# Windowed attention and a squared-ReLU layer on one core: a clamp in the adding instruction, paired squares, V half copies by DMA, and tokens 1024 to 1535 by half-size products

## The chip, the cores and the metric

The kernel runs on one NeuronCore of a Trainium2 chip. The metric is the device time of one execution in microseconds. The engines are named as in the profile: PE is TensorE's matrix products and PEld its weight loads, DVE is VectorE, ACT is ScalarE, POOL is GpSimd, SP is SyncE, which here only issues transfers. Each engine works through its own queue in order, and a wait at the head of a queue holds everything behind it.

## What is computed

The reference, cut to what matters, has two stages. The first is attention in a window of 32 positions to each side, over 8 batches, 8 heads, 576 positions and 64 channels a head. The second is a two-layer network on the 4608 tokens that come out.

```
scores = scale * np.matmul(q, k.transpose(0, 1, 3, 2))
mask = np.abs(pos[:, None] - pos[None, :]) <= 32
attn = softmax of scores where mask
x = (attn @ v), as 4608 tokens x 512
h = x @ w_in                     # 512 -> 2048
r = np.maximum(h, 0.0)
out = ((r * r) @ w_out)          # 2048 -> 512
```

## The kernel before

Attention works through 24 groups of 192 tokens (three to a batch). POOL loads a group's K, Q and V and turns them to bf16 on the way (`load_qk`, L377; `load_v`, L415). The windows of two groups overlap: half of the first V tile of a group equals half of the second tile of the group before. For the 16 groups that are not the first of their batch, that half is copied inside the core, by VectorE (L410) or ScalarE (L412), instead of being loaded.

K and Q have to be turned so that channels lie along the partitions. For the first NTG = 9 groups TensorE does this with products against an identity (`turn_pe`, L463), and VectorE or ScalarE moves the result from PSUM (L476, L477). For the other groups a DMA does it, issued from SP (`turn_dma`, L491). Likewise the result of attention is turned by TensorE for the first NXT = 9 groups (L630, L636, moved by L644 or L646) and by SP's DMA for the others (`xturn`, L649, L652). Between these lie the scores (L531), the exponential by ScalarE (L554), the mask by VectorE (L562), the product with V (L590) and the division (L604, L608). For the first NSPLIT = 6 groups the two windows of a group are masked one by one, for the others together.

The first layer works on 512 tokens at a time, over 2048 columns. Two forms exist. The plain one (`mm1`, L690) does products of 128x192, 128x256 or 128x512 over four slices of the contraction; ScalarE takes max(h, 0) from PSUM to bf16 (L665, or VectorE at L664) and VectorE or ScalarE squares it (L660, L659). It is used for tokens 0 to 1535; tokens 1024 to 1535 come as products of 128x512, in pairs of two PSUM banks (`PAIR`). The other form (`mm1s`, L770) splits tokens, contraction and columns in halves and gets the eight half products from seven (Strassen's scheme in Winograd's form). It needs four differences of the inputs (L742) and of the weights (L730). It is used for the six stretches of 512 tokens from 1536 on, each in four blocks m of 256 + 256 columns. In a block, two banks X and Y take the seven products in the order 1, 2, 6, 5, 7, 3, 4, and the results are taken out in between:

- after product 1 the bank X is copied to Y (L809 or L810);
- after product 2, X holds the first result: `one` takes max(h, 0) (L665) and squares it, 512 wide;
- after products 6 and 5, Y and X are copied to SBUF in fp32 (L670);
- after products 7 and 3, `fused` adds the copy to Y and to X on VectorE and writes bf16 (L794); when both are there, one instruction of 1024 clamps them at zero (L800 on VectorE or L801 on ScalarE) and one squares them;
- after product 4, Y holds the last result: `one` again, 512 wide.

The second layer uses the same scheme of seven products (`strassen`, `product`, L917; its sums at L885, its additions at L949) for all but the first 512 tokens, which go through L835. Some of its blocks, and those of the first layer, begin with a product of zeros over the whole second bank (`wash`, L895), where a mark "w" in the order asks for it. Stores to DRAM go out through SP or ScalarE (L847, L848).

The order of everything is written out by hand in the string ORDER: for each recorded operation an engine letter (P, A, D, G, S) and a due time, and for each buffer a slot. The due times come from a plan and decide only the order in each engine's queue; on the chip every operation starts when its waits are over. While TensorE has nothing to do in the first microseconds it runs products of zeros (`fill`, L299).

Of the kernel before, what the change touches and what calls it, by code (L numbers as in the profile page):

```python
# [2 lines left out]

# [18 lines left out]
    MM1S=(1536, 2048, 2560, 3072, 3584, 4096),  # L22
# [8 lines left out]
    NTG=9,  # L31
# [3 lines left out]
    NXT=9,  # L35
    NSPLIT=6,
# [20 lines left out]
    ALTB=300,  # L57
)
# [170 lines left out]
def dve(n, fast=True):  # L229
    return 153 + (0.52 if fast else 1.04) * n  # L230


class Gen:
# [7 lines left out]
    def alloc(self):  # L241
# [31 lines left out]
        if cfg["MM1S"]:  # L273
            self.SW = [sb(f"sw{i}", [128, 2, 1024], BF16) for i in range(4)]
            self.XS = [sb(f"xs{i}", [128, 2, 256], BF16) for i in range(4)]
# [125 lines left out]
    def load_v(self, b, g, key, after=None):  # L401
        G, NV = 3 * b + g, self.cfg["NV"]
        vt = self.V[G % NV]
        for j in range(2):
            k0 = 192 * g - 32 + 128 * j
            lo, hi = max(k0, 0), min(k0 + 128, S_)
            if self.vcopy(G) and j == 0:
                lo += 64
                vs, vf = self.V[(G - 1) % NV][64:128, 1, :, 0:64], vt[0:64, 0, :, 0:64]
                self.p.rec("DVE", lambda e, vs=vs, vf=vf: e.tensor_copy(vf, vs), reads=[("v", (G - 1) % NV, 1)], writes=[("vc", G % NV)],  # L410
                           key=key + 2, dur=290, name=f"vc{b}{g}",
                           alt=("ACT", act(512), lambda e, vs=vs, vf=vf: e.activation(vf, vs, ACTF.Copy)) if self.cfg["ALT"] else None,  # L412
                           bias=self.cfg["ALTB"])
# [319 lines left out]
    def mm1s(self, t0, key):  # L733
# [5 lines left out]
        b11, b12, b21, b22 = xt[:, 0:2, r:r + 256], xt[:, 0:2, r + 256:r + 512], xt[:, 2:4, r:r + 256], xt[:, 2:4, r + 256:r + 512]  # L739
        for i, a, b, rd in ((0, b12, b11, st[0] + st[1]), (1, b22, xs[0][:], st[1] + [("xs", 0)]),  # L740
                            (2, b22, b12, st[1]), (3, b21, xs[1][:], st[0] + [("xs", 1)])):
            p.rec("DVE", lambda e, o=xs[i][:], a=a, b=b: e.tensor_tensor(o, a, b, ALU.subtract), reads=rd, writes=[("xs", i)],  # L742
                  key=key, dur=dve(512), name=f"xs{i}.{t0}")
        tag = lambda f, h: [("gt", (t0 // 64 + 4 * h + x) % (GRING // 64), d) for x in range(4) for d in f]
        for m in range(4):
# [46 lines left out]
            def fused(src, tg, u, y, kk, nm, hh=hh, add=add):  # L792
                hs = lambda y=y: self.rt(hh)[:, 512 * y:512 * y + 512]
                add.append(p.rec("DVE", lambda e: e.tensor_tensor(hs(), src(), self.oe(u), ALU.add), reads=[tg, u],  # L794
                                 writes=[(hh, y)], key=kk, dur=dve(512, False), name=nm, uses=[v, hh], after=add[0] if y else None))
                if y or not cfg["FP"]:
# [3 lines left out]
                    p.rec("DVE", lambda e: e.tensor_scalar(src2(), src2(), 0.0, None, ALU.max), reads=rd, writes=rd, key=kk, dur=153 + 0.26 * c,  # L800
# [6 lines left out]

            prod(1, ks[0])
# [3 lines left out]
            one(X, xtag, rt, lo, ks[1], f"{t0}.{m}")  # L812
# [80 lines left out]
    def wash(self, e, v):  # L893
        if v.wash:
            e.matmul(self.bank(v, 1), self.ZZ[:, 0:128], self.ZZ[:, 0:512], start=True, stop=True)  # L895
# [190 lines left out]
D900 G1350 A1170 D2200 D5546 D9773 D10213 D10698 D7178 D9553 D11762 D7058 D7598 D10413 D11962 D9453 D5746 D17653 D5256  # L1086
D4966 D1100 D1800 D9993 D10808 D2000 D7378 D9253 D18439 D38379 D42315 D48333 D30870 D48923 S1350 D6458 S900 D4366
G2488 G1700 G4852 G3276 G5640 G4064 G6428 G7956 A1600 A8036 A2050 A7416 G7168 G9388 A14797 G8696 G11052 G10272 G11936
G14196 G17484 G19880 G19100 A20153 G12716 G13408 G20660 G22228 P7128 D7733 P8149 D8701 P9323 A9958 D11076 P10902
A11926 D13121 P12451 D12921 D13806 D14562 P15127 D15742 D16012 P16197 P16768 A17208 P10560 A11112 P11327 D12062 P13044  # L1090
A13769 D15057 P13859 A16107 D17753 P15812 D16698 D16968 A18022 P18772 D19242 D19512 P19032 P20347 D20883 P14284 A15399
P8746 A12954 P16998 A18631 D20198 P19922 A20755 D21967 P21297 D21767 D22653 A23417 P24197 D24667 D24937 P24457 P27062
A27502 G15812 G14976 G18264 G16648 G21440 G29120 P26667 A28812 P31252 D31857 P32967 A33735 D34952 P18112 A19659 P34916
A35551 D37008 P19262 A22922 A24520 P42969 D43856 D44741 D46664 P47949 D48433 D49043 P48634 P50153 D50648 P20637 D23338
P22877 A28317 A31435 P24687 A25557 P27292 D28162 D30990 P31647 D39217 G25324 G26852 G23796 G23008 D48633 G33156 G33848
P45589 A46819 P43229 A43781 P36669 D39839 D41762 P48209 A48844 D49962 P23537 D28715 P50383 A51018 D53131 P27952 A29733
D30318 P51233 D51885 D52155 A53074 P54597 D55067 D55953 P54857 P57743 D58183 P21557 A22427 D33714 D41077 D42415 D43170
D44056 D45979 D55267 D65040 P22217 A24025 A26052 P25347 A26867 D25623 D37694 D26378 D27134 D32476 D36323 D35637 D40391
P26007 A32250 A37979 P32307 A33240 G26112 G24584 G28380 G27640 D52841 G30840 G44088 P45299 A46111 P46795 D47295 P33392
D34399 A36579 P48864 A49872 D51200 P28612 A30940 P50808 A52046 D54369 P30592 D33162 D38664 P53677 D56638 D56908 A57664  # L1100
P58633 D59354 D59624 P61205 P61435 D61875 P39921 A40791 P29932 A42101 D53816 P29272 A32745 P34052 P38193 P40581 P44435
A45509 A84798 P35341 A38794 A41286 P36001 A37484 G31532 G38378 G30004 G35520 G58298 G44876 P55087 A55768 P57348 D58736
P42309 D45426 D47781 P60555 A61415 A62533 D63822 P52153 A53682 P53937 A55274 D62428 P66663 D67167 D68590 A69481 P71217
D72383 D72653 P73101 P74641 D75081 P37329 P41445 P43571 P45931 A47634 A68310 P55482 A56690 P58893 A59763 D63270 P51493
A54177 P57973 A58843 D70796 P59895 D61152 G39214 G34732 G32368 G43300 D62980 G36356 G42416 P59553 D60600 P57006 D57594
P39057 P47085 P49289 P52813 A54672 A92023 P73331 A74201 D81590 P64276 A65136 A66254 D67372 P62529 A63613 P68670 D69275
D69545 D70301 P70957 D71427 D71697 P72641 P72871 D74509 P66923 A70089 A72187 P63403 D65726 P64926 D66481 A67282 P56142
P61665 P65799 P68930 A74695 S89327 P71477 A73215 G64554 G59826 G62094 G46452 D60310 G45760 G75739 P70667 A71479 P72351
D73338 P74871 D76318 D78751 G62834 G48131 G48967 G47295 G65294 G63670 P73991 A75297 A76415 D77533 S67856 S69146 P67797
A68880 P78984 D79454 D80339 D81095 P83561 D84578 D85464 P100060 P100290 D102613 P69794 A70877 D73824 P80107 P80971  # L1110
A82373 D87520 D79654 D86149 D75633 D84778 D82142 P83821 P84695 A85779 P88206 P89080 D96479 A91421 A114133 P89954
P93074 A94158 P94208 P95082 A101298 P100780 P101654 D103165 A111183 P102528 P104052 D106283 A112550 P104926 P105800
A106884 S107575 P75744 P76607 A77681 A95788 G56480 G55692 G66082 G61306 A87456 G75047 G81159 P77471 A78821 A81345
# [112 lines left out]
```

## Time and profile before

| what | value |
|---|---|
| runs of the kernel | 289.16, 287.22, 288.34 us; median 288.34 |
| profiled execution | span 287.0 us from the first to the last instruction; the page gives no other time of it |
| instructions | 7773 |
| granted TensorE clock, mean | 0.999 |
| first-layer seven-product blocks | 24, with 672 products of 128x256 (L770) |
| plain first-layer products | 256 of 128x192, 64 of 128x256, 59 records of 128x512 (L690) |

The profiled execution's span is 1.3 us under the median of the runs, which also count what lies around the span. A row of a group names line, engine, operation, the tiles written and read, their shapes and the count; then the busy time in us and the mean duration of one in ns; then how long the engine stood idle just before them and on what. A row of the stages gives, for each stretch of the span, the busy time and the instruction count of each engine, the granted clock of TensorE, the DMA share and the rate. Matrix products overlap, so their durations (some 273 ns for one of 128x256) are longer than the distance from one to the next.

### The profile page before, as it was taken

To read this page: it belongs to the slowest core of one execution; us is meant where nothing else is said; L and a number is where in the kernel's file an instruction comes from. 1 tells how busy PE (TensorE), PEld (TensorE's weight loads), DVE (VectorE), ACT (ScalarE), POOL (GpSimd) and SP (SyncE) were. 2 spreads that over 40 slices of the span, in tenths; PEclk is the share of its full clock that TensorE was granted. 3 is DMA by queue.
4 is the path that set the end of the run, shared out by engine and by line. 5 is a ranking of instruction groups with operands and counts; after the bars stand their busy time and mean duration, and the time that the engine had idled before them with its cause. 6 is when DMAs were issued, how large, how long until landed. Compare 5 with 4: busy or idle time off the path is not lost.

```text
span 287.0 us, 7773 instructions
## 1 busy us (share of the span) xinstructions
PE 279.1 (97%) x3137; PEld 234.6 (82%) x3151; DVE 238.0 (83%) x438; ACT 215.7 (75%) x328; POOL 115.0 (40%) x153
## 2 busy tenths in 40 slices
PE   8999999999999999998999999999999999999995
PEld 8879866787756688886898888888888888888884
DVE  4787797989887798996899989998989978898721
ACT  2787666857868787887887889988887688798620
POOL 8999867194498052076235912605000000000000
PEclk9999999999999999999999999999999999999999
DMA  9999999999999999999999996989941612200233
GB/s 143 165 193 185 204 173 156 156 113 152 119 158 175 190 112 147 190 115 163 163 154 134 151 166 144 132 180 118 145 98 46 130 34 61 75 0 2 73 112 110
DMA packets 162915, 37.57 MB, mean 131 GB/s; under 512 B 150080, under 2 KB 162368, under 8 KB 162880
## 3 DMA queue, kind: packets, MB, share of 16 engines
q0 software_dynamic: 113728, 17.93, 87.7%
q1 hardware_dynamic: 44432, 15.34, 29.8%
q10 hardware_dynamic: 4720, 3.80, 5.1%
q8 instruction: 25, 0.41, 0.6%
q14 instruction: 10, 0.08, 0.1%
HBM read 36.70 MB, written 9.44 MB: 161 GB/s over the span
## 4 chain that ended last, share of the span: by engine, by line
PE 78%; DMA 10%; POOL 6%; DVE 2%; issue 2%; ACT 1%; ACTq 0%; DVEq 0%; POOLq 0%
PE ps L917 31%; PE ps L770 24%; PE ps L690 9%; PE ps L835 4%; POOL raw L377 4%; PE ps L590 3%; DMA w<-in_moe_w_in_dram 3%; PE ps L531 3%; DMA kq<-raw 3%; DMA v<-in_v_dram 2%; POOL v L415 2%; DMA xt<-xa 2%; PE ps L463 1%; DVE rt L794 1%; PE ps L630 0%
## 5 line engine op out<-in xcount | busy, mean ns | idle before, releaser
L665 ACT ACTIVATE rt<-ps 128x512 bf16<-128x512 f32 (+2 forms) x81 | 48.4, 606 | 17.6 <-PE ps L690 7.3
L670 ACT ACTIVATE oe<-ps 128x512 f32<-128x512 f32 x72 | 42.0, 595 | 22.2 <-PE ps L917 15.1
L554 ACT ACTIVATE e<-ps 128x1024 bf16<-128x1024 f32 x48 | 48.8, 1022 | 6.8 <-PE ps L531 5.0
L377 POOL DMA_DIRECT2D raw<-in_q_dram x46 | 36.7, 809 | 42.3 <-DMA kq<-raw 39.0
L377 POOL DMA_DIRECT2D raw<-in_k_dram x46 | 36.8, 816 | 27.2 <-DMA kq<-raw 20.8
L917 PE MATMUL ps<-w,gt 128*128 128x256 bf16 x384 | 47.0, 273 | 0.0
L690 PE MATMUL ps<-xt,w 128*128 128x192 bf16 (+2 forms) x379 | 46.4, 271 | 0.6 <-DMA w<-in_moe_w_in_dram 0.2
L415 POOL DMA_DIRECT2D v<-in_v_dram x48 | 38.6, 814 | 12.4 <-ACT v L412 10.0
L917 PEld LDWEIGHTS ps<-w,gt 128*128 128x128 bf16 x384 | 36.6, 98 | 4.9 <-issue 0.2
L770 PE MATMUL ps<-xs,sw 128*128 128x256 bf16 x288 | 39.9, 272 | 0.0
L690 PEld LDWEIGHTS ps<-xt,w 128*128 128x128 bf16 x384 | 32.4, 98 | 8.8 <-ACT v L412 0.3
L659 ACT ACTIVATE gt<-rt 128x512 bf16<-128x512 bf16 (+2 forms) x51 | 38.7, 777 | 0.3
L794 DVE TENSOR_TENSOR rt<-ps,oe 128x512 bf16<-128x512 f32 x48 | 32.9, 688 | 5.1 <-PE ps L770 3.8
L917 PE MATMUL ps<-ts,gt 128*128 128x256 bf16 x256 | 31.9, 273 | 0.0
L562 DVE TENSOR_TENSOR pt<-e,mask 128x2048 bf16<-128x2048 bf16 (+1 forms) x30 | 30.2, 1007 | 1.9 <-ACT e L554 1.4
L917 PE MATMUL ps<-ts,ss 128*128 128x256 bf16 x256 | 31.7, 273 | 0.0
L770 PEld LDWEIGHTS ps<-xs,sw 128*128 128x128 bf16 x288 | 27.4, 98 | 3.3 <-ACT oe L670 0.2
L770 PE MATMUL ps<-xt,w 128*128 128x256 bf16 x192 | 27.2, 273 | 0.2
L917 PEld LDWEIGHTS ps<-ts,ss 128*128 128x128 bf16 x256 | 24.7, 98 | 3.2
L660 DVE TENSOR_TENSOR gt<-rt 128x1024 bf16<-128x1024 bf16 (+2 forms) x49 | 26.4, 557 | 0.8 <-ACT rt L665 0.7
L917 PEld LDWEIGHTS ps<-ts,gt 128*128 128x128 bf16 x256 | 24.5, 98 | 3.2 <-DVE oe L949 0.3
L770 PEld LDWEIGHTS ps<-xt,w 128*128 128x128 bf16 x192 | 18.1, 98 | 3.3 <-ACT ps L809 0.4
(70 smaller groups left out, 405.2 us busy)
## 6 DMA issues: line engine op xcount, KB each, us to landing
out_dram<-oe SPq DMA_DIRECT2D x23, 256.0 KB, 3.5
out_dram<-oe ACTq DMA_DIRECT2D x13, 256.0 KB, 4.4
v<-in_v_dram POOLq DMA_DIRECT2D x16, 128.0 KB, 5.5
w<-in_moe_w_in_dram POOLq DMA_DIRECT2D x4, 512.0 KB, 9.8
w<-in_moe_w_out_dram POOLq DMA_DIRECT2D x4, 512.0 KB, 16.4
raw<-in_q_dram POOLq DMA_DIRECT2D x18, 96.0 KB, 5.3
raw<-in_k_dram POOLq DMA_DIRECT2D x14, 112.0 KB, 5.3
raw<-in_q_dram POOLq DMA_DIRECT2D x14, 112.0 KB, 6.9
```

Source lines behind the costliest of these rows:

```text
L377: self.p.rec("POOL", lambda e, j=j, dst=dst: e.dma_start(dst, s[j]), writes=[self.rtag(t, b, g, j)], dma=(f"{t}{G % self.cfg['NRAW']}{j}", ...
L415: self.p.rec("POOL", lambda e, j=j, lo=lo, hi=hi, k0=k0: e.dma_start(vt[lo - k0:hi - k0, j, :, 0:64], self.v[b, :, lo:hi, :].rearrange("h ...
L554: last = self.p.rec("ACT", lambda e, ef=ef, v=v: e.activation(ef(), self.bank(v, 0, 2), ACTF.Exp, scale=0.125), reads=[v], writes=tags, ke ...
L562: self.p.rec("DVE", lambda e, pf=pf, ef=ef, mb=mb, n=n: e.tensor_tensor(pf(y=0, n=n), ef(y=0, n=n).rearrange("p (w h q) -> p w h q", w=n, ...
L659: alt = ("ACT", act(c), lambda e: e.activation(dst, src(), ACTF.Square)) if self.cfg["ALT"] else None
L660: self.p.rec("DVE", lambda e: e.tensor_tensor(dst, src(), src(), ALU.mult), reads=rd, writes=wr, key=key, dur=dve(c), name=name, alt=alt, ...
L665: return self.p.rec("ACT", lambda e: e.activation(dst(), src(), ACTF.Relu), reads=rd, writes=wr, key=key, dur=act(c), name=name, alt=alt, ...
L670: self.p.rec("ACT", lambda e: e.activation(dst(), src(), ACTF.Copy), reads=rd, writes=wr, key=key, dur=act(c), name=name, alt=alt, bias=se ...
L690: mm = e.matmul(ht[:, n * x:n * x + n], self.W1[:, ft, 128 * d:128 * d + 128], self.XT[:, ft, r:r + n], start=(ft == 0 and x == 0), stop=( ...
L770: mm = e.matmul(bk[:, 256 * x:256 * x + 256], lhs(k, 256 * m + 128 * x), rhs[:, k, :], start=start and x == 0 and k == 0, stop=(k == 1), s ...
L794: add.append(p.rec("DVE", lambda e: e.tensor_tensor(hs(), src(), self.oe(u), ALU.add), reads=[tg, u], writes=[(hh, y)], key=kk, dur=dve(51 ...
L917: mm = e.matmul(op[:, 256 * y:256 * y + 256], lhs[:, l0[0] + k, a:a + 128], rhs[:, r0 + k, c0:c0 + 256], start=start and y == 0 and k == 0 ...
```

## The change

It has seven parts, and a new ORDER over all of them, of which the diff shows the first line; the old one has two marks "w", the new one has one.

1. **Clamp inside the addition** (`AS`): the addition of `fused` becomes VectorE's TENSOR_ADD_SAT, which computes max(min(a + b, s0), s1) with s0 the largest fp32 number and s1 = 0. The clamping instruction goes.
2. **Squares in pairs** (`ZP`): a block's first result (`one`, after product 2) shares a buffer with the sum after product 7, and the sum after product 3 shares one with the last result (after product 4). Each pair is squared by one instruction of 1024. Before there were squares of 512, 1024 and 512.
3. **Merged differences** (`XM`): two of the four input differences become one instruction of 1024.
4. **V half copies by DMA** (`VD`): the 16 copies are transfers issued from SP, of 64 partitions with their padding columns, instead of copies by VectorE or ScalarE.
5. **Tokens 1024 to 1535** go from the plain form to the seven-product form.
6. **Group 8, the ninth,** has K, Q and its result turned by SP's DMA (NTG and NXT from 9 to 8).
7. **Groups 3 to 5** have both windows scored and masked together (NSPLIT from 6 to 3).

A wider block (`wide`) comes with the change but is not called (`WIDE=()`); it is left out here.

```diff
-    MM1S=(1536, 2048, 2560, 3072, 3584, 4096),
+    MM1S=(1024, 1536, 2048, 2560, 3072, 3584, 4096),
-    NTG=9,
+    NTG=8,
-    NXT=9,
-    NSPLIT=6,
+    NXT=8,
+    NSPLIT=3,
+    AS=1,
+    VD=1,
+    ZP=1,
+    XM=1,
+    WIDE=(),
...
+            self.XSA = sb("xs", [128, 4, 2, 256], BF16)
+            self.XS = [self.XSA[:, (0, 2, 1, 3)[i], :, :] for i in range(4)]
...
+                if self.cfg["VD"]:
+                    vs, vf = self.V[(G - 1) % NV][64:128, 1, :, :], vt[0:64, 0, :, :]
+                    self.p.rec("SP", lambda e, vs=vs, vf=vf: e.dma_start(vf, vs), reads=[("v", (G - 1) % NV, 1), ("vset", (G - 1) % NV), ("vset", G % NV)],
+                               writes=[("vc", G % NV)], dma=(f"vc{G % NV}", G), key=key + 2, dur=450, move=(4, 60), name=f"vc{b}{g}",
+                               slack=self.cfg["TSLACK"])
-                self.p.rec("DVE", lambda e, vs=vs, vf=vf: e.tensor_copy(vf, vs), reads=[("v", (G - 1) % NV, 1)], writes=[("vc", G % NV)],
...
+        if cfg["XM"]:
+            both = [bass.AP(xt, o, [[4 * RING, 128], [x, 2], [RING, 2], [1, 256]]) for o, x in ((r + 256, 2 * RING), (r, 256))]
+            p.rec("DVE", lambda e: e.tensor_tensor(self.XSA[:, 0:2, :, :], both[0], both[1], ALU.subtract), reads=st[0] + st[1],
+                  writes=[("xs", 0), ("xs", 2)], key=key, dur=dve(1024), name=f"xs0.{t0}")
...
+            def pair(z, y, src, tg, u, kk, nm, held, v=v, lo=lo, hi=hi):
+                zf = lambda: self.rt(z)[:, 512 * y:512 * y + 512]
+                if u is None:
+                    held.append(self.relu(zf, src, [tg], [(z, y)], kk, "r" + nm, 512, uses=[v, z], after=held[0] if y else None))
+                else:
+                    held.append(p.rec("DVE", lambda e: e._custom_dve(TENSOR_ADD_SAT, out=zf(), in0=src(), in1=self.oe(u), s0=3.4028234e38, s1=0.0),
+                                      reads=[tg, u], writes=[(z, y)], key=kk, dur=dve(512, False), name=nm, uses=[v, z], after=held[0] if y else None))
+                if y:
+                    o = 256 if u is None else 0
+                    dst = bass.AP(gt, lo[0] * GRING + rg + o, [[16 * GRING, 128], [(hi[0] - lo[0]) * GRING + 256 - 2 * o, 2], [GRING, 2], [1, 256]])
+                    self.square(lambda: self.rt(z).rearrange("p (y d t) -> p y d t", y=2, d=2), dst, [(z, 0), (z, 1)],
+                                tag(lo, int(o > 0)) + tag(hi, int(o == 0)), kk, "g" + nm, 1024, uses=[z])
...
             prod(2, ks[1])
-            one(X, xtag, rt, lo, ks[1], f"{t0}.{m}")
+                pair(za, 0, X, xtag, None, ks[1], f"{t0}.{m}", ha)
...
             prod(7, ks[4])
-            fused(Y, ytag, p5, 0, ks[4], f"c22.{t0}.{m}")
+                pair(za, 1, Y, ytag, p5, ks[4], f"c22.{t0}.{m}", ha)
             prod(3, ks[5])
-            fused(X, xtag, u2, 1, ks[5], f"c12.{t0}.{m}")
+                pair(zb, 0, X, xtag, u2, ks[5], f"c12.{t0}.{m}", hb)
             prod(4, ks[6])
-            one(Y, ytag, rt2, hi, ks[6], f"{t0}.{m}b")
+                pair(zb, 1, Y, ytag, None, ks[6], f"{t0}.{m}b", hb)
...
 ORDER = """
-D900 G1350 A1170 D2200 D5546 D9773 D10213 D10698 D7178 D9553 D11762 D7058 D7598 D10413 D11962 D9453 D5746 D17653 D5256
...
+D850 G850 A22521 D3755 D1300 D2605 D3555 D4665 D1500 D3115 D8849 D4775 D8729 D5880 D10316 D4895 D1900 D15584 D4375
...
```

More of the change, by code (lines that the diff above doesn't have):

```diff
@@ L2 @@
 from concourse import mybir
+from concourse.dve_ops import TENSOR_ADD_SAT
 ALU = mybir.AluOpType
@@ L744, in mm1s @@
         tag = lambda f, h: [("gt", (t0 // 64 + 4 * h + x) % (GRING // 64), d) for x in range(4) for d in f]
+        if t0 in cfg["WIDE"]:
+            for m in range(2):
+                self.wide(t0, key + 4 * m, m, (b11, b21, b22), st, tag)
+            return
         for m in range(4):
@@ L894, in wash @@
         if v.wash:
-            e.matmul(self.bank(v, 1), self.ZZ[:, 0:128], self.ZZ[:, 0:512], start=True, stop=True)
+            for i in range(v.n // 2, v.n):
+                e.matmul(self.bank(v, i), self.ZZ[:, 0:128], self.ZZ[:, 0:512], start=True, stop=True)
     def product(self, g, i, key, v):
@@ L1091 @@
[L1091 to L1110, printed above, removed]
```

272 lines of the change are left out of this document (188 added, 84 removed), and 11 rows, old and new, of the table ORDER.

## The prediction

> **What bounds the kernel now.** I read the page first (its busy times), then the busy time by stage, the waits of TensorE, the chain of waits, and last the groups of instructions with the shapes kept apart.
>
> ```profile
> span 287.0 us, 7773 instructions
> PE 279.1 (97%) x3137; PEld 234.6 (82%) x3151; DVE 238.0 (83%) x438; ACT 215.7 (75%) x328; POOL 115.0 (40%) x153
> ```
> ```profile
> core 0: us, PE busy (x) PEld busy (x) DVE busy (x) ACT busy (x) POOL busy (x), PEclk, DMA share, GB/s
> 20.00:80.00 60.00, 59.38 (x750) 46.89 (x756) 51.43 (x101) 44.02 (x67) 40.53 (x54) 1.00 1.81 158
> 80.00:110.00 30.00, 29.18 (x300) 20.75 (x302) 25.88 (x43) 23.53 (x29) 18.31 (x24) 1.00 1.82 157
> 110.00:140.00 30.00, 28.54 (x308) 24.47 (x306) 26.03 (x47) 24.09 (x38) 10.31 (x13) 1.00 1.56 151
> 140.00:283.00 143.00, 142.88 (x1489) 125.24 (x1490) 121.44 (x207) 111.61 (x180) 26.85 (x35) 1.00 0.77 105
> 180.00:190.00 10.00, 10.00 (x116) 8.70 (x114) 9.23 (x16) 9.40 (x16) 3.79 (x5) 1.00 1.79 134
> ```
> ```profile
> PE ps L770 <- DVE rt L794: 1.3, 1, 1.3
> ```
> ```profile
> 11.65 9.21 DMA w<-in_moe_w_in_dram
> 37.84 2.59 PE ps L835 x12
> 126.16 5.83 DMA xt<-xa
> 246.94 9.61 PE ps L770 x88
> 265.28 18.35 PE ps L917 x168
> ```
>
> TensorE is the bound. From 20 to 283 us it is idle 0.62 + 0.82 + 1.46 + 0.12 = 3.0 us, at full granted clock (1.00). Its one wait of weight, 1.3 us, lies where the chain passes through a transpose that landed late (126.16, 5.83 us): VectorE stood waiting for it with an addition behind. VectorE and ScalarE are both busy, but after 140 us they keep TensorE waiting for next to nothing. So an instruction taken from them there pays nothing by itself; a product taken from TensorE pays in full. A busy TensorE is not one at its peak, so I price products by their spacing in the chain: 128x512 products cost 2.59/12 = 215.8 ns, 128x256 products 9.61/88 = 18.35/168 = 109.2 ns.
>
> **The change part by part: TensorE.**
>
> ```profile
> L690 PE MATMUL ps<-xt,w 128*128 128x512 bf16 x59 | 14.2, 379 | 0.4 <-issue 0.2
> L895 PEld LDWEIGHTS ps<-zz 128*128 128x128 bf16 x2 | 0.2, 98 | 0.0
> ```
> ```profile
> 70.81 0.42 PEld L463 LDWEIGHTS ps<-ident,raw 80*128 80x128 bf16 x8
> 72.49 0.42 PEld L463 LDWEIGHTS ps<-ident,raw 80*128 80x128 bf16 x8
> 100.50 0.42 PEld L630 LDWEIGHTS ps<-ident,xa 128*128 128x128 bf16 x4
> 100.89 0.27 PEld L636 LDWEIGHTS ps<-ident,xb 128*128 128x128 bf16 x4
> ```
>
> - Tokens 1024 to 1535: 16 column tiles x 4 = 64 products of 128x512 go (the group shows 59, some records being missing), 64 x 215.8 ns = 13.81 us. In come 4 blocks x 7 products x 4 = 112 of 128x256, 112 x 109.2 ns = 12.23 us: **-1.58 us**.
> - Of the two washing products (L895, a 128x512 each) one mark "w" is left in the new order: **-0.2 us**.
> - The ninth group (number 8): 16 turns of K and Q go (70.81 and 72.49: 0.42 us of weight loads per eight, the last 98 ns of each overlapping what follows, so some 0.33 us; 0.65 together) and 8 turns of its result (from 100.50 to 100.89 + 0.27 less one load, some 0.5; gaps in it put the true price nearer 0.4): **-1.05 us**, with 0.8 and 1.2 as ends.
>
> TensorE sum: -2.83 us. The two scores of groups 3 to 5 in one piece leave the products as they are.
>
> **VectorE and ScalarE.**
>
> ```profile
> L801 ACT ACTIVATE rt<-rt 128x1024 bf16<-128x1024 bf16 x8 | 8.4, 1055 | 1.0 <-DVE rt L794 1.0
> L800 DVE TENSOR_SCALAR rt<-rt 128x1024 bf16<-128x1024 bf16 x16 | 6.9, 440 | 0.2
> L794 DVE TENSOR_TENSOR rt<-ps,oe 128x512 bf16<-128x512 f32 x48 | 32.9, 688 | 5.1 <-PE ps L770 3.8 <-ACT oe L670 0.4 <-ACT gt L659 0.2
> L660 DVE TENSOR_TENSOR gt<-rt 128x1024 bf16<-128x1024 bf16 x21 | 14.2, 683 | 0.0
> L660 DVE TENSOR_TENSOR gt<-rt 128x512 bf16<-128x512 bf16 x18 | 7.2, 417 | 0.0
> L412 ACT ACTIVATE v<-v 64x512 bf16<-64x512 bf16 x9 | 5.6, 622 | 1.0 <-DMA v<-in_v_dram 0.9
> L410 DVE COPY v<-v 64x512 bf16<-64x512 bf16 x7 | 2.0, 290 | 0.2
> L665 ACT ACTIVATE rt<-ps 128x1024 bf16<-128x1024 f32 x8 | 8.2, 1023 | 2.5 <-PE ps L690 2.4
> L670 ACT ACTIVATE oe<-ps 128x512 f32<-128x512 f32 x72 | 42.0, 595 | 22.2 <-PE ps L917 15.1 <-PE ps L770 4.8 <-PE ps L835 0.9
> L742 DVE TENSOR_TENSOR xs<-xt 128x512 bf16<-128x512 bf16 x12 | 4.9, 419 | 1.7 <-DMA xt<-xa 1.7
> ```
>
> Out: the clamps, 8.4 + 6.9 = 15.3 us; the V copies, 5.6 + 2.0 = 7.6 us; per block two squares of 417 and one of 683 become two of 683, 151 ns x 24 = 3.6 us. In: the block work of tokens 1024 to 1535. Before, 8 x (1023 + 683) = 13.6 us; after, 4 x (five passes of some 595, two additions of 688, two squares of 683) = 22.9 us, and three differences, one of 1024 at about the 683 of L660 and two of 419, 1.5 us: +10.8 us. The merged differences of the other groups, the three merged masks and the turned-out evacuations of group 8 each save under 2.5 us more. Net some -16 to -20 us of 453.7.
>
> The addition that also clamps is not in this trace. The nearest row with its operands is the plain addition, 688 ns; the far end is addition plus clamp in VectorE, 688 + 440/2 = 908 ns per addition, where the fusing saves nothing. I take 688. At 908 its 56 additions would cost 12.3 us more, and VectorE would still have room after 140 us (121.44 of 143), so either end is worth nothing on the path. What is saved here pays only through waits of TensorE: between 0 and the 3.0 us of idle time above. I take **-0.9 us**, near the lower end: half of the 1.3 us wait (VectorE's queue before an addition gets shorter, but a late transpose remains late) and a tenth of the rest.
>
> **V copies by DMA, and the SP queue.**
>
> ```profile
> DMA to landing us min/median/max: 2.3/3.6/7.1
> ```
> ```profile
> 14.54 0.63 ACT L412 ACTIVATE v<-v 64x512 bf16<-64x512 bf16 x1
> 20.86 0.56 DVE L646 COPY xt<-ps 128x768 bf16<-128x768 bf16 x1
> 25.02 2.14 PE L690 MATMUL ps<-xt,w 128*128 128x192 bf16 x24
> 159.31 2.33 POOL L415 DMA_DIRECT2D v<-in_v_dram  x3
> 194.23 0.43 PE L590 MATMUL ps<-v,pt 128*128 128x65 bf16 x8
> ```
> ```profile
> SPq L210 <- DMA raw<-in_k_dram: 81.6, 6, 58.3
> ```
> ```profile
> POOL v L415 <- ACT v L412: 10.0, 1, 10.0
> ```
> ```profile
> q0 software_dynamic: 113728, 17.93, 87.7%
> ```
>
> The transfers of xt, also from SP and inside the core, land after 2.3 to 7.1 us, 3.6 in the middle; a copy took 0.63 us at most. So a V half comes 1.7 to 6.5 us later after its source landed, middle 3.0. Later that is hidden: the loads issued from 159.31 on serve a product of 194.23. The tight place is the start: the copy of 14.54 leads to the evacuation that ends at 21.42, and TensorE needs that only after the first 8 of the 24 products from 25.02, about 25.7 us; before that the products wait for the weights anyway (chain, 11.65 + 9.21). Cover 4.3 us: I take **0**, with +2.2 us as the far end.
>
> SP issues in order. It gets 16 copies and 4 transposes of group 8, and each copy waits for a V load of POOL's; behind it stand the transposes and stores. That SP stands long before a load is nothing new (81.6 us in six waits) and cost TensorE nothing. POOL's next load into a V buffer also waits for the copy that reads it (10.0 us once, with ScalarE as the copier); a copy 3.0 us later holds POOL's queue so much longer, against loads issued some 30 us ahead. I cost all this at 0 in the sum; without that cover it is rival 1.
>
> Sum: -1.58 - 0.2 - 1.05 - 0.9 = -3.7 us. The page gives no time beside the span of 287.0; the median of the runs, 288.34, stands 1.3 above it, which start and end I take as unchanged. So span 283.3, **time 284.6 us**.
>
> **The rivals.**
>
> 1. *Transposes late behind a V copy in SP's queue.* One late transpose cost 1.3 us of TensorE here. Two more of them, not foreseen in the order, give back 2.7: 287.3 us; from three on the gain is gone. For it: POOL's loads take 87.7% of the DMA engines' span, and landings spread threefold. Against: of TensorE's waits in this trace a single one of weight came from a late transpose.
> 2. *Evacuation becomes the bound while tokens 1024 to 1535 run (80 to 110 us); this ends slower than before.* VectorE and ScalarE are busy 25.88 + 23.53 = 49.4 of 60 us there; +10.8, less some 1.8 of V copies, gives 58.4, or 97%. If they reach only the share of 140 to 283 us (233.05 of 286, 81.5%), the stage needs 35.8 us instead of 30: +5.8, time 290.4. It turns into a loss if they stay under 87% (33.7 us). Against: from 180 to 190 us they ran at 93% with TensorE busy 10.00 of 10, and the new blocks can spread into 110 to 140 us, where clamps and copies go.
> 3. *More of the idle time goes:* all 3.0 us instead of 0.9: 282.5 us. For it: both engines that empty PSUM get emptier; against: much of the idle time has DMA behind it.
> 4. *Half-size products cost more than counted,* because each needs its own weights: 112 loads instead of 64. Not overlapped at all they would cost 98 + 109 ns each, 23.2 us instead of 12.2, time 295.6; the point from which the split loses is 13.81/112 = 123 ns. Against: PEld busy 125.24 beside PE 142.88 in 143 us, and 109.2 ns in runs of 88 and 168 products.
>
> [...]
>
> **How the numbers follow.** Forecast 0.58 (its own range 283.4 to 286.0), rival 1 0.18, rival 2 0.09, rival 3 0.12, rival 4 0.03. The range of 8 in 10 takes in rivals 1 and 3 with the bounds of the V copies and leaves out 2 and 4: 282.6 to 288.0. A measurement of this kernel tells about 1% from no change: under 285.5 is faster. That is rival 3 and some five sixths of the forecast, 0.60; within 1% the rest of it, rival 1 and a third of rival 2, 0.31; slower 0.09.
>
> **What would show it.** Right: some 784 products of 128x256 in the first layer's split line, none of 128x512 from the plain one; no clamps; 56 clamping additions of about 690 ns; TensorE idle no more than 3 us after 20 us. Each step has its sign of failure: additions over 900 ns; a TensorE wait on VectorE or ScalarE summing to over 2 us between 80 and 115 us (rival 2); TensorE or VectorE waiting for xt or kq behind a V copy in SP's queue (rival 1); a product behind its V copy in the first 30 us. The prediction is wrong if TensorE's idle time grows by more than the 2.8 us taken from its work.

## The result, and the profile after

The changed kernel is slower: 299.69 us in the median (297.67 to 301.61, four runs) against 287.78 us (286.7 to 289.16) for the kernel before on the same chip, a ratio of 1.0418 with a 95% interval of 1.0355 to 1.0481. The forecast was 284.6 us. The profiled execution took 300.6 us, 2.0 more than its span. An execution that took over 1.5% longer than the fastest of its kernel is left out of the medians and ratios here and below (one of six in e6, two of four in e10, one of six in e17), while the expectations name e6 and e10 by the medians of all their executions, 292.8 and 297.4 us.

The page of the kernel after, its engines and granted clock, and then its busy time in the stretches shown of before, with the first 20 us ahead of them:

```profile
span 298.6 us, 7824 instructions
PE 278.6 (93%) x3155; PEld 239.3 (80%) x3163; DVE 236.2 (79%) x408; ACT 206.6 (69%) x305; POOL 114.4 (38%) x153
```
```profile
core 0: us, PE busy (x) PEld busy (x) DVE busy (x) ACT busy (x) POOL busy (x), PEclk, DMA share, GB/s
0.00:20.00 20.00, 15.42 (x262) 14.09 (x262) 12.33 (x45) 9.48 (x11) 19.04 (x30) 1.00 1.58 168
20.00:80.00 60.00, 58.12 (x749) 47.31 (x749) 50.38 (x93) 46.23 (x70) 43.28 (x58) 1.00 1.97 171
80.00:110.00 30.00, 26.92 (x298) 23.23 (x296) 25.13 (x38) 23.95 (x34) 16.02 (x21) 1.00 1.92 150
110.00:140.00 30.00, 24.63 (x266) 19.65 (x267) 19.71 (x32) 14.66 (x21) 17.01 (x22) 0.89 1.76 194
140.00:283.00 143.00, 141.15 (x1482) 124.25 (x1481) 124.77 (x199) 109.32 (x165) 19.03 (x25) 1.00 0.72 94
```

TensorE was idle for 287.0 - 279.1 = 7.9 us before and for 298.6 - 278.6 = 20.0 us now. The 12.1 us more are the whole loss, for the spans differ by 11.6. Half of it, 6.2 us, lies in 80 to 140 us, where VectorE and ScalarE are idle for longer too: from 110 to 140 us ScalarE's busy time fell from 24.09 to 14.66 us. So no engine is the bound there; the chain below shows what they wait for, transfers above all. POOL issued 22 loads in that stretch instead of 13. Another 3.1 us lie in the first 20, of which before has this row:

```profile
0.00:20.00 20.00, 18.48 (x297) 16.90 (x297) 13.24 (x44) 11.80 (x17) 19.05 (x29) 1.00 1.62 164
```

What TensorE waited for (total, times, longest), and the pieces of the chain of waits that are transfers or follow one:

```profile
PE ps L603 <- DMA v<-v: 6.2, 3, 4.3
PE ps L1046 <- DVE oe L1078: 2.1, 2, 1.2
PE ps L793 <- ACT oe L683: 1.4, 1, 1.4
```
```profile
12.13 5.30 DMA v<-v
62.05 9.80 DMA kq<-raw
105.67 5.36 DMA v<-v
118.90 5.79 DMA xt<-xa
125.83 7.65 DMA out_dram<-oe
276.99 18.35 PE ps L1046 x168
```

The product with V (L603) waits 6.2 us for V copies (`v<-v`): at the start, and at 107 us for a copy that SP issued at 105.67 and that landed 5.36 us later. Between them a transpose of K and Q took 9.80 us. After that wait, and once more from 135 us on, TensorE is granted half its clock for some 3.4 us (0.50 from 112 to 114 us and from 135 to 138), so that the granted clock is 0.83 in the mean of ten:

```profile
core 0: us, PE busy (x) PEld busy (x) DVE busy (x) ACT busy (x) POOL busy (x), PEclk, DMA share, GB/s
110.00:120.00 10.00, 8.66 (x98) 7.01 (x98) 6.72 (x12) 4.18 (x6) 5.63 (x8) 0.83 1.79 195
120.00:130.00 10.00, 8.54 (x114) 7.13 (x113) 7.61 (x14) 5.51 (x9) 9.07 (x12) 1.00 1.90 206
130.00:140.00 10.00, 7.43 (x62) 5.51 (x63) 5.38 (x8) 4.96 (x8) 2.31 (x3) 0.83 1.59 181
```

Groups of the kernel after that answer to terms of the sum, and its landings:

```profile
L841 DVE CUSTOM_DVE_ANT_0 rt<-ps,oe 128x512 bf16<-128x512 f32 x56 | 37.5, 686 | 7.7 <-PE ps L793 5.2 <-ACT oe L683 1.4 <-ACT gt L672 0.3
L793 PE MATMUL ps<-xs,sw 128*128 128x256 bf16 x336 | 45.6, 273 | 1.4 <-ACT oe L683 1.4
L1024 PEld LDWEIGHTS ps<-zz 128*128 128x128 bf16 x1 | 0.1, 98 | 0.0
```
```profile
raw<-in_k_dram POOLq DMA_DIRECT2D x16, 96.0 KB, 7.5
v<-v SPq DMA_DIRECT2D x16, 66.0 KB, 5.3
kq<-raw SPq DMA_TRANSPOSE x32, 7.3
```

### The profile page after: what moved, and what is told of

Read it like the earlier page. It is cut to its first block, busy times and chain, and to the rows that moved or that the text cites. A ratio compares the mean times of both kernels' runs of the same rounds, so it can differ in the third digit from the quotient of the medians.

```text
span 298.6 us, 7824 instructions
## 1 busy us (share of the span) xinstructions
PE 278.6 (93%) x3155; PEld 239.3 (80%) x3163; DVE 236.2 (79%) x408; ACT 206.6 (69%) x305; POOL 114.4 (38%) x153
## 4 chain that ended last, share of the span: by engine, by line
PE 73%; DMA 17%; DVE 5%; ACT 2%; issue 2%; SPq 1%; POOL 0%; ACTq 0%; DVEq 0%
PE ps L1046 28%; PE ps L793 27%; PE ps L703 6%; DMA v<-v 4%; DMA kq<-raw 3%; PE ps L963 3%; PE ps L603 3%; DMA out_dram<-oe 3%; DMA raw<-in_q_dram 2%; PE ps L544 2%; DMA ts<-in_q_dram 2%; DMA xt<-xa 2%; PE ps L476 2%; DMA xt<-xb 1%; DVE pt L575 1%
## 5 line engine op out<-in xcount | busy, mean ns | idle before, releaser
L683 ACT ACTIVATE oe<-ps 128x512 f32<-128x512 f32 x76 | 44.2, 597 | 22.9 <-PE ps L1046 14.4
L678 ACT ACTIVATE rt<-ps 128x512 bf16<-128x512 f32 (+1 forms) x77 | 42.3, 563 | 21.2 <-PE ps L793 10.8
L1046 PE MATMUL ps<-w,gt 128*128 128x256 bf16 x384 | 49.5, 278 | 0.2 <-ACT ps L1087 0.2
L793 PE MATMUL ps<-xs,sw 128*128 128x256 bf16 x336 | 45.6, 273 | 1.4 <-ACT oe L683 1.4
L841 DVE CUSTOM_DVE_ANT_0 rt<-ps,oe 128x512 bf16<-128x512 f32 x56 | 37.5, 686 | 7.7 <-PE ps L793 5.2
L672 ACT ACTIVATE gt<-rt 128x1024 bf16<-128x1024 bf16 (+1 forms) x44 | 43.2, 1000 | 0.5
L793 PEld LDWEIGHTS ps<-xs,sw 128*128 128x128 bf16 x336 | 31.9, 98 | 5.9 <-ACT oe L683 1.7
L793 PE MATMUL ps<-xt,w 128*128 128x256 bf16 x224 | 32.4, 278 | 2.4 <-issue 1.5
L703 PE MATMUL ps<-xt,w 128*128 128x192 bf16 (+1 forms) x320 | 31.7, 251 | 0.0
L603 PE MATMUL ps<-v,pt 128*128 128x65 bf16 x384 | 19.7, 194 | 7.0 <-DMA v<-v 6.2
## 6 DMA issues: line engine op xcount, KB each, us to landing
w<-in_moe_w_in_dram POOLq DMA_DIRECT2D x4, 512.0 KB, 10.1
```

What stands on the lines that cost most here:

```text
L603: mm = e.matmul(ps[z:z + n, c:c + 65], ptt[:, 4 * (h % 2) + h // 2, z:z + n], vt[:, w, h, 0:65], start=((w == 0 or (z == 64 and split)) an ...
L672: alt = ("ACT", act(c), lambda e: e.activation(dst, src(), ACTF.Square)) if self.cfg["ALT"] else None
L678: return self.p.rec("ACT", lambda e: e.activation(dst(), src(), ACTF.Relu), reads=rd, writes=wr, key=key, dur=act(c), name=name, alt=alt, ...
L683: self.p.rec("ACT", lambda e: e.activation(dst(), src(), ACTF.Copy), reads=rd, writes=wr, key=key, dur=act(c), name=name, alt=alt, bias=se ...
L703: mm = e.matmul(ht[:, n * x:n * x + n], self.W1[:, ft, 128 * d:128 * d + 128], self.XT[:, ft, r:r + n], start=(ft == 0 and x == 0), stop=( ...
L793: mm = e.matmul(bk[:, 256 * x:256 * x + 256], lhs(k, 256 * m + 128 * x), rhs[:, k, :], start=start and x == 0 and k == 0, stop=(k == 1), s ...
```

## The experiments

**Theories.** A: the V copies come late, because they stand in SP's in-order queue and take some 5.3 us to land. B: group 8's transposes crowd the DMA engines. C: the work on tokens 1024 to 1535 makes VectorE and ScalarE the bound. Later two more for what A left: D1, SP's time for issuing; D2, the new order lets POOL load 20 to 50 us earlier, and the loads crowd out urgent transfers.

| run | kernel | median us | ratio to before (95%) |
|---|---|---|---|
| e1 | after, V copies on the engines | 295.99 | 1.0303 (1.0261 to 1.0346) |
| e2 | before, V copies by DMA | 297.43 | 1.0351 (1.0296 to 1.0405) |
| e4 | after, V copies earlier in SP's queue | 300.37 | 1.0454 (1.0374 to 1.0534) |
| e5 | before, clamp in the addition | 286.49 | 0.9981 (0.9964 to 0.9999) |
| e6 | before, clamp, merged differences, pairs | 292.24 | 1.0205 (1.0178 to 1.0233) |
| e7 | before, group 8 by DMA | 288.04 | 1.0046 (1.0015 to 1.0076) |
| e8 | e1, 10 stores from ScalarE | 301.23 | 1.0491 (1.0452 to 1.0531) |
| e9 | e1, loads later and held | 289.62 | 1.0098 (1.0079 to 1.0118) |
| e10 | after, loads later and held | 295.04 | 1.0271 (1.0221 to 1.0322) |
| e11 | before, clamp, merged differences | 286.64 | 0.9991 (0.9973 to 1.0009) |
| e12 | e9, two transposes earlier | 289.12 | 1.0064 (1.0040 to 1.0087) |
| e13 | e9 without the holding | 296.27 | 1.0313 (1.0272 to 1.0353) |
| e14 | e9, pairs undone | 293.49 | 1.0239 (1.0213 to 1.0264) |
| e15 | e10, copies from ScalarE's queue | 295.52 | 1.0304 (1.0277 to 1.0331) |
| e16 | e2, first batch on ScalarE | 293.88 | 1.0242 (1.0200 to 1.0283) |
| e17 | e12, the two after groups 12 and 13 | 290.68 | 1.0115 (1.0067 to 1.0163) |

In the same sessions the kernel before took 286.7 to 287.2 us, and each difference from it below is taken within its session. No kernel beats it by more than e5's 0.2%.

### The V copies

**e1.** `VD=1` becomes `VD=0`; the 16 copies get due times 0.9 us (first batch) or 2.5 us ahead of their product. One load of POOL is also due 4.1 us later, at 180 us.

> The changed kernel (299.7 us) with one of its seven parts undone: the 16 V half copies are instructions of VectorE or ScalarE again, due 2.5 us before the product with V that needs them (0.9 us in the first batch); all else keeps its place. Theory A, the copies stand late in SP's in-order queue and land some 5.3 us after their issue: the two long waits for a copy (5.3 us on the chain at 12 us and 5.4 us at 105 us), with the lower clock behind the second, go, so 286 to 290 us. Theory B, the DMA engines as a whole are overloaded by the change (group 8's transposes above all): the copies' 1024 packets of 166371 are no relief, only the start's 1.5 us comes back, 297 to 299 us. Theory C, the new work on tokens 1024 to 1535 makes VectorE and ScalarE the bound: they get 7.6 us of copies more, so 299 us or over.

Measured 295.99 us. 3.7 of the 12 us come back, as neither A nor B alone said. C expected 299 us or over, for VectorE and ScalarE get work back here, and falls. With the copies gone, TensorE waits at about the same place for something else:

```profile
PE ps L544 <- DMA kq<-raw: 4.4, 1, 4.4
```

**e2.** The kernel before with `VD=1`, due times 5.5 us ahead of the product (earlier in the first batch).

> The kernel before (287.8 us) with this one part of the change: the 16 V half copies by DMA from SP, due 5.5 us before the product with V (in the first batch as soon as their source is due). Theory A: the start loses 1.5 us as in the changed kernel, and each later copy that SP or the DMA engines bring over 5.5 us late costs TensorE a wait: 289.5 to 294 us. Theory B: the copies are too small to matter, 287.5 to 289.5 us. Theory C: the same as B, or some tenths less, since the engines lose 7.6 us of copies.

Measured 297.43 us, far beyond the range of A: this one part makes the kernel before as slow as nearly the whole change. TensorE's waits, a piece of the chain and two rows of SP's timeline (start, length, the instructions) tell why:

```profile
PE ps L603 <- DMA v<-v: 7.6, 5, 4.6
```
```profile
14.34 6.84 DMA v<-v
```
```profile
72.75 11.35 SPq L504 DMA_TRANSPOSE kq<-raw  x5
84.15 0.69 SPq L418 DMA_DIRECT2D v<-v  x1
```

At the start the copy is 6.84 us on the chain, and TensorE waits 4.6 us for it. The 16 copies land after 3.7 us in the median here, so it is not their middle that costs. At 84 us SP had been held by transposes that waited for their loads; the copy behind them left late and landed 4.23 us later.

**e16.** As e2, but `if self.cfg["VD"] and b:`, so that the first batch's two copies stay on ScalarE.

> The kernel before with the V copies by DMA from SP as in the run that came to 297.4 us (+10.2), but the first batch's two copies on ScalarE again. In that run the first two were followed by waits of TensorE of 4.7 us and smaller ones before 25 us, some 6.8 us in all; a wait of 2.1 us and the lower clock behind it came at 86 us. If these add up: 290 to 292 us. If the later copies are then hit elsewhere: over 293 us.

Measured 293.88 us: some 3.5 us of the 10.2 were the first batch, 6.8 are the other 14 copies. TensorE's waits for them:

```profile
PE ps L603 <- DMA v<-v: 4.9, 2, 2.7
```

**e4.** In the changed kernel, due times in us of the copies on SP that move by over 5 us (ten; the expectation counts eight):

```
group  4: 44.62 -> 39.40    group 10:  96.57 -> 68.35    group 11:  98.27 -> 70.81    group 13: 103.46 -> 89.96
group 14: 118.60 -> 99.71   group 16: 143.42 -> 118.09   group 17: 140.43 -> 121.90   group 19: 150.57 -> 136.58
group 20: 182.23 -> 160.31  group 23: 195.30 -> 183.33
```

> The changed kernel with the 16 copies still by DMA from SP, but eight of them moved forward in SP's queue, to 13 us after the due time of the load that brings their source (the one behind the wait at 105 us is due at 68.35 instead of 96.57). Theory A: the wait at 105 us and the lower clock behind it go, some 6 to 8 us; the start's 1.5 us and the waits for out and xt partly stay: 291 to 295 us. If the copies now hold SP while their loads are still out, transposes behind them come late and part is given back: up to 298 us. Theory B and C: 298 to 301 us.

Measured 300.37 us, no gain and where B and C had it. The 4.3 us wait for the copy at 107 us went, and one of 5.5 us for K and Q, ten us later, took its place:

```profile
PE ps L544 <- DMA kq<-raw: 6.0, 2, 5.5
```

That is the point at which A alone falls: TensorE waits for another transfer instead, and the time stays. What makes all of them late had to be found.

### SP's issuing or the loads

**e8.** e1 with ten stores issued from ScalarE instead of SP (letter `S` to `A` in ORDER; the expectation counts eleven).

> The changed kernel with V copies on the engines again (296.0 us as measured) and 11 stores of the outputs (units 2 to 12) issued by ScalarE instead of SP. Theory D1, what is left of the loss is SP's own time for issuing: it issues for 53.7 of the 60 us from 90 to 150 us (40.7 before), and 11 stores of some 0.54 us less let the transposes of K and Q leave earlier: 292.5 to 294.5 us. Theory D2, the loss is that loads issued 20 to 50 us earlier than before crowd the DMA engines (landings of K and Q 15 us instead of 5 from 115 to 145 us): no help from the stores' place, 295 to 297 us.

**e9.** e1 with the loads of ORDER later by the rule in the expectation, and

```diff
+        pace = sorted((o for o in self.out if o.eng == "PE"), key=lambda o: (o.start, o.i))
+        for op in self.out:
+            if op.eng == "POOL" and op.dma is not None and 50000 < op.start:
+                op.order.add([o for o in pace if o.start + o.dur <= op.start][-1])
```

> The changed kernel with V copies on the engines again (296.0 us) and POOL's loads from 50 us on due later: not before their due time in the kernel before, but 11 us (K, Q) or 16 us (V) ahead of their first use in the plan at the latest, and each held until the TensorE instruction that the plan has just ahead of it is done. Work, transposes and stores are unchanged. Theory D2 (crowding by early loads): landings from 115 to 145 us come back to some 5 to 8 us, the 4.4 us wait for a transpose of K and Q at 113 us goes, 290 to 293.5 us. Theory D1 (SP's issuing): no change, 295 to 297 us. If loads now come too late, over 297 us with TensorE waiting behind loads.

e8 came to 301.23 us, above both expectations and 5 slower than e1 (TensorE still waits 6.4 us for K and Q, and 4.7 for an addition). e9 came to 289.62, 6.4 faster and just under D2's range. So D2 holds, and D1 isn't what those 6.4 us were: by the sum of SP's DMA instructions it issues for some 50 of the 60 us from 90 to 150 us in e9, hardly less than the some 54 in e1, and for 47 in e8, which is slower than both. (That the stores now hold ScalarE in e8 is not ruled out.) Issues from 115 to 145 us in before, e1 and e9, with the median time to landing as the last column:

```profile
raw<-in_k_dram POOLq DMA_DIRECT2D x3, 112.0 KB, 4.7
...
kq<-raw SPq DMA_TRANSPOSE x7, 5.3
```
```profile
raw<-in_k_dram POOLq DMA_DIRECT2D x3, 112.0 KB, 15.6
...
kq<-raw SPq DMA_TRANSPOSE x6, 8.2
```
```profile
raw<-in_k_dram POOLq DMA_DIRECT2D x3, 112.0 KB, 5.2
...
kq<-raw SPq DMA_TRANSPOSE x8, 5.9
```

Loads of the same size take 15.6 us to land in e1, where they leave early, and 5.2 in e9, where they are held; the transposes of K and Q in the same stretch go from 8.2 to 5.9. The wait of 4.4 us for K and Q is down to 2.2 (line numbers are five higher in e9; the row names VectorE's `xa`, but a transpose of K and Q that left SP at 107.86 us, behind one that had waited for `xa`, landed at the same moment, 114.3 us):

```profile
PE ps L549 <- DVE xa L626: 2.2, 1, 2.2
```

**e13.** e9 without the four lines above.

> The kernel that came to 289.6 us (V copies on the engines, loads later) without the holding: the loads have the same order in POOL's queue, but each leaves as soon as its buffer is free. If the order in the queue alone keeps the DMA engines uncrowded, as it did in the kernel before: 288.5 to 291 us. If the holding did it: back to 293 to 296 us, with landings over 10 us again.

Measured 296.27 us: the queue's order alone gives nothing, only with the holding is the gain there. From 115 to 145 us the loads of K and Q land after 6.7 to 12.6 us again, and TensorE waits 4.1 us for K and Q. What sets the four kernels apart is when the loads leave: from 110 to 120 us POOL issues none in the kernel before, 11 in e1, 9 in e13 and 2 in e9. Over 110 to 140 us the counts differ less (13, 22, 16 and 17), so it seems to be their bunching just ahead of the wait that counts. Holding at the old due times wasn't tried.

**e10.** The changed kernel, V copies on SP, with e9's order of loads and holding; five loads of V are due earlier than in e9, since a copy needs them earlier.

> The changed kernel itself (299.7 us), V copies by DMA from SP, with one thing undone: POOL's loads from 50 us on stand later and are held to the plan, in the same way that took the kernel with its V copies on the engines from 296.0 to 289.6 us. If early loads that crowd the DMA engines were most of the loss and the copies come late mainly because of the crowd: 290 to 292 us. If the copies cost the same 3.7 us with and without the crowd: 293 to 294.5 us. If copies behind loads that now come later hold SP longer, and with it the transposes: 295 to 300 us.

Measured 295.04 us (293.3 to 296.2 by the interval of the ratio). That rules out the first expectation only, for the interval reaches into the second. The copies cost 5.4 us where the loads are held (against e9) and 3.7 where they are not (after against e1); with these intervals the two are not told apart. So holding the loads doesn't make the copies harmless. The first 20 us of e10 and of e9 show one place:

```profile
0.00:20.00 20.00, 15.01 (x254) 13.75 (x254) 12.37 (x45) 9.23 (x11) 19.05 (x29) 1.00 1.59 166
```
```profile
0.00:20.00 20.00, 17.73 (x285) 16.09 (x286) 13.73 (x47) 11.13 (x13) 19.04 (x30) 1.00 1.60 169
```

TensorE is busy 2.7 us less there. Another is near 190 us. SP's timeline in e10, the piece of the chain and VectorE's wait there, and then the same part of SP's timeline in e9:

```profile
183.51 1.22 SPq L670 DMA_TRANSPOSE xt<-xb  x1
184.84 0.52 SPq L423 DMA_DIRECT2D v<-v  x1
185.46 0.54 SPq L981 DMA_DIRECT2D out_dram<-oe  x1
186.09 1.29 SPq L670 DMA_TRANSPOSE xt<-xb  x1
```
```profile
186.09 5.69 DMA xt<-xb
```
```profile
DVE xs L760 <- DMA xt<-xb: 3.4, 1, 3.4
```
```profile
182.18 1.21 SPq L670 DMA_TRANSPOSE xt<-xb  x1
183.49 0.53 SPq L981 DMA_DIRECT2D out_dram<-oe  x1
184.12 1.28 SPq L670 DMA_TRANSPOSE xt<-xb  x1
```

The copy puts 0.6 us between the two transposes, and SP was 1.3 us late already. The second one lands 3.5 us later than in e9 (191.78 against 188.24), VectorE waits 3.4 us for it with an addition of the second layer behind, and TensorE waits for that addition. So rival 1 (a transpose late behind a V copy) does occur; but the copy's 0.6 us is the smaller part of the delay.

**e15.** e10 with the copies' `"SP"` changed to `"ACT"`, same due times.

> The kernel with the V copies by DMA and the loads later and held (297.4 us), the 16 copies issued from ScalarE's queue instead of SP's at the same due times. If SP's queue is the cause (a copy stands behind transposes there, and transposes behind a copy that waits for its load): 290 to 293 us, the start's loss of some 2 us excepted. If the landing of the copies is (5 us after issue, whoever issues): 295 us or over. If ScalarE is now held by copies whose loads are out, also 295 us or over, with waits for ScalarE.

Measured 295.52 us, no gain over e10's 295.04, where SP's queue as the cause would give 290 to 293. From ScalarE the copies take as long, and TensorE waits for four of them:

```profile
v<-v ACTq DMA_DIRECT2D x16, 66.0 KB, 5.1
```
```profile
PE ps L608 <- DMA v<-v: 4.6, 4, 1.6
```

So the landing counts for more than whose queue it is: it takes 5.1 us from ScalarE here, 4.7 from SP in e10 and 5.3 from SP in the changed kernel.

### The other parts, and what is left

**e5.** The kernel before with `AS=1`.

> The kernel before with only the clamp inside the adding instruction: 24 clamping instructions less (15.3 us of VectorE and ScalarE), every other place in the order kept. By all theories the engines off the path are relieved and TensorE waits a little less: 286.8 to 287.8 us. If the new instruction cost what addition and clamp cost before (908 ns), VectorE would lose what ScalarE gains, and the time would be 287.5 to 288.5 us.

**e11.** The same with `XM=1`.

> The kernel before with the clamp in the addition and the merged differences, without the pairs of squares. The kernel with all three came to 292.8 us, the one with the clamp alone to 286.5. If the pairs are the cause (they hold buffers and results longer): 286 to 287 us. If the merged difference is (it needs all 512 tokens' transposes before any of it starts): 289 us or over.

**e6.** The same with `ZP=1` as well; ORDER was mended by hand for the merged squares.

> The kernel before with the three parts that relieve VectorE and ScalarE and no others: clamp in the addition, merged differences, and squares in pairs (not for tokens 4096 to 4607, whose four blocks would need more buffers than there are). Order, V copies, group 8 and tokens 1024 to 1535 as before. If the change's loss comes from V copies, transfers and the new order (theories A and D below), these parts are harmless: 286 to 287.5 us, that is -0.3 to -1.2. If the pairs hold PSUM banks or buffers longer than the singles did and that is part of the loss, over 288 us.

**e14.** e9 with `ZP=0`, mended by hand the other way.

> The kernel that came to 289.6 us (V copies on the engines, loads later and held), with the pairs of squares undone: 28 blocks have squares of 512, 1024 and 512 again (some 151 ns more of engine time a block, 4.2 us in all); the clamp in the addition stays. In the order of the kernel before, the pairs cost 6 us. If they do so in the changed kernel's own order, and make up what is left of the gap to the forecast of 284.6: 285 to 287.5 us. If that order was made for the pairs and they cost nothing there: 289.5 to 291 us.

The clamp gave 0.7 us (e5 at 286.49, a little under its range); with the merged differences added, the gain is not told from nothing (e11: 0.9973 to 1.0009). The pairs cost some 5.6 us where they were put into the order of before (292.24 in e6 against 286.64 in e11), and undoing them cost 3.9 us in the order that was made with them (293.49 in e14, above both expectations). Both changes were made in an order not made for them, so the pairs' own cost stays open.

**e7.** The kernel before with `NTG=8, NXT=8`.

> The kernel before with group 8 alone turned by DMA (two transposes of K and Q, two of the result, from SP), its K and Q loads moved some 5 to 9 us forward so that they are there. My prediction's step: TensorE loses 1.05 us of work, so 286.2 to 287 us. Theory B, group 8's transposes crowd the DMA engines and make later transposes late: 288.5 us or over.

Measured 288.04 us, between the two expectations: 1.3 slower (0.15 to 0.76%), though PE busy fell from 279.1 to 277.6 us in its profile. That leaves little for B, but in this order the step brings no gain. Tokens 1024 to 1535 by themselves in the old order weren't tried.

**e12** and **e17** move group 14's two transposes in e9, to 88 us and to 94 us.

> The kernel that came to 289.6 us (V copies on the engines, loads later and held), with the transposes of K and Q of group 14 due at 88 instead of 101 and 104 us, in the 11 us in which SP otherwise waits for a result of attention, and their loads some 7 to 10 us earlier. If the wait that is left at 112 us is SP's queue between 90 and 112 us, it goes: 286 to 288 us. If another transpose takes its place, 288.5 to 290 us.

> As the kernel that came to 289.1 us (V copies on the engines, loads later and held, K and Q of group 14 loaded earlier), but group 14's two transposes stand in SP's queue behind those of groups 12 and 13, which in that run came late in their place, and ahead of the results of groups 8 and 9. If the last place where TensorE waits, between 100 and 120 us, is only the order of these few transposes in SP's queue: 286 to 287.5 us, no slower than the kernel before. If SP, which issues for 25 of the 30 us there, cannot serve them all whatever the order: 288.5 to 290 us.

Measured 289.12 us (e12) and 290.68 us (e17, 288.61 to 292.49, a little above its second range). The wait at 112 us that e9 has left moves from one transpose to the next: in e12 TensorE waits 2.1 us for K and Q at 103 us, in e17 2.2 us at 110 us, behind a transpose of `xa` that left at 105.3 and took 5.9 us. So it isn't the order of these few. SP's issuing as such remains the likely reason there (in e12 it makes up 39% of the chain from 96 to 118 us, by the transposes of K and Q), but no run takes work off SP in e9's kernel.

## Why the prediction was wrong

- **The step that failed: "V copies by DMA, and the SP queue", taken at 0 with +2.2 us as the far end.** It is 10.2 us by itself in the kernel before (e2) and 3.7 to 5.4 in the changed one. Three things were mis-sized. The cover was the first: 4.3 us at the start was counted up to the evacuation's use, but in TensorE's order the product with V stands long before that. The trace of the kernel before has this product in the first row below: it starts 0.8 us after the copy's end at 15.17, so the cover was 0.8 us. In e2 the same product waited 4.6 us. The landing was the second: 3.6 us in the middle, taken from transposes of xt, fits the kernel before (3.7 in e2), but the first copy, the one without cover, took 6.84 there, near the far end of the rows (7.1), and in the changed kernel the middle is 5.3. The third was the price of one late transfer: 1.3 us in rival 1, taken from a single row; in the kernel after one wait of 4.3 us was followed by a granted clock of 0.50 from 112 to 114 us.
- **What had no term: the order itself.** I priced seven parts as if each went into the old order. In the new one loads leave earlier, 22 of POOL's instructions from 110 to 140 us instead of 13, and holding them is worth 6.4 us without the V copies by DMA (e1 to e9) and 4.7 us with them (after to e10). The sum had SP's and POOL's queues at 0, because loads issued 30 us ahead looked like slack; but where they left early the urgent transposes landed late (8.2 us in e1, 5.9 in e9, from 115 to 145 us). By e13 it isn't their place in POOL's queue but the free buffers that let them go early; why buffers come free earlier in the new order is not shown.
- **TensorE sum, -2.83 us: the counts came out** (784 products of 128x256, one washing product; 18.35 us for 168 products, as before, so 109.2 ns). PE busy fell by only 0.5 us, since two stretches of 3.4 us at half clock took, by estimate, some 3.4 us back; in e17, where no such stretch comes ahead of the end, it is 276.2 (below), 2.9 less than before. As time it was never seen: idle time ate it.
- **Clamping addition 688 ns:** 686. **Relief -0.9 us** (its own working, half of 1.3 and a tenth of the other 1.7, gives 0.8): -0.7 with the clamp alone. The other parts of the relief don't bear it out, for with the merged differences the gain is not told from nothing, and with the pairs the time rose.
- **Group 8, -1.05 us:** as work about right (1.5 in e7's profile), as time +1.3.
- **Rival 1** named one of the mechanisms (e10, at 186 us), with a chance of 0.18 and too small a price. **Rival 2** falls: from 80 to 100 us in e9 TensorE is busy 20.00 of 20 (below). **Rivals 3 and 4** fall with the idle time and the 109.2 ns.

The rows are, in this order, the product with V in the kernel before, e17's engines, and 80 to 100 us of e9:

```profile
15.98 0.41 PE L590 MATMUL ps<-v,pt 128*128 128x65 bf16 x8
```
```profile
PE 276.2 (96%) x3163; PEld 237.6 (82%) x3163; DVE 238.5 (83%) x415; ACT 211.4 (73%) x314; POOL 114.5 (40%) x153
```
```profile
80.00:100.00 20.00, 20.00 (x222) 17.40 (x220) 18.07 (x29) 17.09 (x25) 14.78 (x19) 1.00 1.96 157
```

The prediction's own mark of being wrong, TensorE's idle time growing by over 2.8 us, was met: 12.1. The copies and the early loads together make 10.1 us (after to e9). Undone in one order they are 3.7 and 6.4 us (by e1), in the other 5.4 and 4.7 (by e10), so neither is the larger for certain. With both undone, e9 is still 2.9 us over the kernel before. The forecast was 3.7 us under it, so 6.6 us are missing. In e9's profile a wait of 2.2 us at 112 us and the half clock after it (by estimate 1.7) are the largest part. Why K and Q of that group can't come sooner is not settled.

## What to carry to other kernels

Moving a small copy from an engine that had room to a DMA exchanged 0.29 us of VectorE or 0.62 us of ScalarE for a landing of 3.7 us (e2) to 5.3 us (the kernel after) in the median: count the latency up to the first instruction that needs it in its engine's order. When a change brings a new order, compare the loads' issue times as well as the instruction counts: with the loads early (e1) transposes of K and Q landed after 8.2 us, with the loads held (e9) after 5.9. Here, holding loads to the consumer's pace rather than letting free buffers decide was worth 4.7 to 6.4 us of some 296 to 300.

## What the runs showed of the hardware

- In the kernel after, the granted clock fell to 0.50 for some 3.4 us behind a wait of 4.3 us (0.50 from 112 to 114 us), so by estimate that wait cost about 6 us (4.3 and half of 3.4). It fell so again from 135 us on (0.50 to 138 us), behind several waits of at most 1.5 us each, and in e9 behind one of 2.2 us (0.50 from 116 to 118 us), while one of 2.7 us in e16 left the clock at 1.00. What decides is not shown.
- A load of 112 KB took 4.7 us to land in the kernel before, 15.6 in e1 and 5.2 in e9, at nearly the same rate of bytes (162, 174 and 182 GB/s), all from 115 to 145 us.
